# Attention and a noisy top-2 router with eight experts in one kernel: the router of two groups two slots earlier, weight loads re-timed, four experts per half before the halves alternate

## The chip, the cores and the metric

The kernel runs on one core of one Trainium2 chip. The metric is the device time of one execution in microseconds. Before the change the median of 14 runs is 454.57 us (450.78 to 479.65). One further execution was recorded by the profiler; it took 454.08 us, of which 452.3 us lie between its first and its last instruction (the span). All times inside the kernel below are counted from the start of that span.

Engine names in the profile: PE is the matrix engine (PEld its weight loads), ACT the scalar engine, DVE the vector engine, POOL the GpSimd engine, SP the sync engine. A trailing q (SPq, POOLq) is the engine's instruction queue, where DMAs are issued.

## The reference: what is computed

Two stages, one after the other. First causal attention in blocks of 64 over 8 batches, 8 heads, 576 positions and 64 channels. Its output is read as 4608 tokens of 512 channels. Then a mixture of experts: for each token two matrix products with 512x8 matrices give logits and a noise scale, the two largest of the 8 noisy logits are kept, and their softmax gives two weights. Each token goes through its two experts (512 to 1024, ReLU, 1024 to 512), and the two results are added with those weights.

```python
logits = x @ w_gate
noise_scale = np.log1p(np.exp(x @ w_noise))
noisy_logits = logits + noise_scale * noise
top2 = np.argpartition(-noisy_logits, 2, axis=1)[:, :2]
...
h = np.maximum(x[mask] @ w1[e], 0.0)
out[mask] += top2_w[mask, k, None] * (h @ w2[e])
```

## The kernel before, in words

**Attention.** The 8 batches form four groups of two (group 0 to 3). A group has 26 score units (UG = 26). One unit is a few PE matmuls into a PSUM tile and one exponential on ACT (`score_unit`, L284, the exponential at L301 or L312). Around each unit the kernel runs what was put on that slot's list: transposes of q and k, products with v (`av_tile`, L323, normalised on DVE at L362 and L363), transposes of the result, steps of the router, DMA issues. A slot is thus one unit: slots 0 to 103 are the four groups. The lists are filled with `at(slot, function, arguments)` and emptied with `run(slot)`. Each engine receives its instructions in the order in which they are written here, and works through them in that order.

**Router.** `router(g)` (L387) is a chain of 16 steps of small DVE instructions, three small ACT instructions and two PE matmuls (L439, L440). It finds for each token of a group its two experts and a free row in each expert's table. The list `rsl` (L767) gives the slot of every step, counted from the start of the next group (r0 = 26 g + 26); `r1` says when the group's scatters begin.

**Scatter.** `scatter(g, j)` (L499) is an indirect DMA issued by POOL. It writes 128 tokens to their rows in `xd`, an internal tensor in HBM with a table of 640 rows for each expert. There are two such tensors, one for each half of the tokens: groups 0 and 1 are half 0, groups 2 and 3 half 1. Each group has 18 scatters (9 token tiles, two experts), which may start only after the last paced instruction (`pace`) of their slot.

**Experts.** The work after attention is 16 blocks, `SEQ`, each one half with one expert. Before the change these are (half 0; experts 0, 1, 2), (half 1; experts 0, 1, 2), and then the halves in turn for experts 3 to 7. So block 3 is the first of half 1. `load_x` (L518) is a transposing DMA on SP's queue that brings the 640 rows of a block into SBUF (tile xg, for block 0 tile xa). It waits until all 36 scatters of its half have landed. `load_rec` (L527) brings the rows' records (destination, weights), and `read_rec` (L536) decodes them on DVE. `layer1` (L570) is 8 steps of 8 matmuls and one ReLU on ACT, `layer2` (L584) 5 tiles of 8 matmuls. In the PE's order the first layer-1 step of the next block stands ahead of layer 2 of this one. A token's first expert writes its result to `yd` in HBM (ACT's queue, L596), its second expert fetches that back with `gather` (L612, POOL, indirect), adds its own on DVE (L599) and sends the sum to the output with an indirect DMA (L601, POOL).

**Slots of the experts.** Slots from 104 on count the steps of the blocks: slots 104 to 110 hold the rest of group 3, block 0 has slots 111 to 124, block 1 has 125 to 137, block 2 begins at 138, and each later block has 13. Group 3's scatters stand at slots 118 to 135.

**Weights.** `load_w` (L219) brings one expert's two matrices in four DMAs of 512 KB, issued by POOL. The loads of experts 0 to 2 stand at fixed slots (L796, L797, L813); from expert 3 on they are issued during the blocks, as listed in `WL` (L822 to L825).

**The queues.** POOL issues q, k, v and weight loads, scatters, gathers and output writes in one order. Eight semaphores serve its DMAs in turn, so each DMA it issues first waits for the landing of the eighth before it. SP issues the clearing of `xd`, the transposing loads and the records in one order.

Of the kernel before, what the change touches and what calls it, by code (L numbers as in the profile page):

```python
# [19 lines left out]
def kernel(  # L20
# [37 lines left out]
    LT = (0, 1, 2, 3, 3, 4, 5, 5)  # L58
# [5 lines left out]
    UG = 2 * UN  # L64
# [25 lines left out]
    wE = main.enter_context(tc.tile_pool(name="wE", bufs=2))  # L90
# [6 lines left out]
    top = main.enter_context(ExitStack())  # L97
# [116 lines left out]
    def v_loads(g):  # L214
        return [(load_v, g, jt) for jt in range(4)] + [(load_v, g, 4, hf) for hf in range(2)]
# [3 lines left out]
    def load_w(pool, e, k=None):  # L219

        if k in (None, 0, "a"):
            wload[e] = (pool.tile([P, DB, F], BF16, tag="w1", name="w1sb"),
                        pool.tile([P, FB, Dm], BF16, tag="w2", name="w2sb"))
        for i, (t, src) in enumerate(zip(wload[e], (moe_w1[e], moe_w2[e]))):
            n = t.shape[1]
            w = src.rearrange("(b p) c -> p b c", p=P)
            if k is None or k == "ab"[i]:
                nc.gpsimd.dma_start(out=t, in_=w)
            elif k in (2 * i, 2 * i + 1):
                b0 = (k % 2) * n // 2  # L230
                nc.gpsimd.dma_start(out=t[:, b0:b0 + n // 2], in_=w[:, b0:b0 + n // 2])
# [286 lines left out]
    def load_x(b):  # L518
        half, e = SEQ[b]
        assert len(scat[half]) == 2 * TH  # L520
        xg = ffn["x"].tile([P, DB, CAP], BF16, tag="xg", name="xg") if b else xa
        ins = nc.sync.dma_start_transpose(out=xg, in_=xd[half][e * CAP:(e + 1) * CAP, 0:Dm])
        for nm in scat[half]:
            tc.add_manual_dep(ins.ins, nm, SYNC_DEP, reason="rows landed")
        xgs[b] = xg
# [99 lines left out]
    GJ = (2, 3, 4, 6, 7)  # L625
    GS = (2, 3, 5, 6)


    E1 = 3
    SEQ = [(h, e) for h in range(NH) for e in range(E1)]  # L630
    for e in range(E1, E):
        SEQ += [(0, e), (1, e)]
    NB = len(SEQ)
    todo = {}

    def at(slot, fn, *args):
        todo.setdefault(slot, []).append((fn, args))

    def run(slot):

        def rank(item):
            fn, args = item
            if fn is router_step:
                return 3 if rgen_n.get(args[0], 0) in (0, 1, 2, 8, 14, 15) else 0
            return {av_tile: 1, transpose_qk: 2, x_transpose: 2}.get(fn, 4)

        items = todo.pop(slot, [])
        while items:
            items.sort(key=rank)
            fn, args = items.pop(0)  # L650
            fn(*args)
# [52 lines left out]
    def read_flags():  # L704
        rs["over"] = nc.values_load(flag_i[0:1, 0:1], min_val=0, max_val=1)

    def warm():

        tp = tr_ps.tile([P, 4, P], F32, tag="tr")
        nc.tensor.matmul(out=tp, lhsT=ident, rhs=ident.unsqueeze(1).to_broadcast([P, 4, P]),  # L710
                         start=True, stop=True)
# [26 lines left out]
    for g in range(NG):  # L738
        s0 = g * UG
        last = g == NG - 1  # L740

        for nm, ch, i in (("q", 1, 0), ("k", 1, 2), ("k", 2, 4), ("q", 2, 6), ("k", "4A", 7), ("q", "4A", 8),
                          ("q", 3, 10), ("k", 3, 12)):
            at(s0 + i, transpose_qk, g, nm, ch)
        if not last:
            for nm, ch, i in (("q", 0, 14 if g else 19), ("k", 0, 17 if g else 22), ("q", "4B", 22), ("k", "4B", 21)):
                at(s0 + i, transpose_qk, g + 1, nm, ch)
            for i, (fn, *a) in enumerate(v_loads(g + 1)):
                at(s0 + 9 + i, fn, *a)
        if g == 0:  # L750
            at(s0 + 13, load_qk, 1, (2,))
            at(s0 + 16, load_qk, 1, (3,))
        if g == 0:
            for i, t in enumerate(((0, 6, 5), (1, 5), (6, 9))):
                at(s0 + 20 + 4 * i, load_tiles, 2, "q", *t)
                at(s0 + 21 + 4 * i, load_tiles, 2, "k", *t)
        elif g == 1:
            at(s0 + 14, load_tiles, 3, "q", 0, TG)
            at(s0 + 17, load_tiles, 3, "k", 0, TG)
        for i, a in enumerate((15, 16, 17, 18, 18, 19, 20, 21, 22, 23)):  # L760
            at(s0 + a, av_tile, g, 0, *((i,) if i < 8 else (8, i - 8)))
        r0 = s0 + UG
        if not last:
            avs = (0, 1, 1, 3, 4, 4, 5, 6, 7, 8)
            xts_ = (3, 5, 7, 9, 10)
        if g < 2:
            rsl = (11, 11, 12, 13, 14, 15, 16, 17, 19, 20, 21, 22, 23, 24, 25, 26)  # L767
            r1 = 26
        elif g == 2:
            rsl = (11, 11, 12, 13, 13, 14, 15, 16, 18, 19, 19, 20, 20, 21, 22, 22)  # L770
            r1 = 23
        else:
            avs, xts_ = (0, 0, 1, 1, 2, 2, 3, 3, 4, 4), (2, 3, 4, 5, 5)
            rsl = (5, 6, 6, 7, 7, 8, 8, 9, 10, 10, 11, 11, 12, 12, 13, 13)
            r1 = 14
        for i in range(TG + 1):
            at(r0 + avs[i], av_tile, g, 1, *((i,) if i < 8 else (8, i - 8)))
        for j in range(5):
            at(r0 + xts_[j], x_transpose, g, j)
        for j in range(RSTEPS):  # L780
            at(r0 + rsl[j], router_step, g)
        for j in range(2 * TG):
            at(r0 + r1 + (2 * j // 3, j, 4 * j // 5, j)[g], scatter, g, j)
# [10 lines left out]
    at(2 * UG + 4, clear_x, 1, 2 * UG + 3)  # L794
    for k in range(4):
        at(2 * UG + 1 + 2 * k, load_w, wE, 0, k)  # L796
        at(2 * UG + 20 + k, load_w, wE, 1, k)  # L797
    for u in (*range(2 * UG + 20, 2 * UG + 24), *range(3 * UG + 14, NG * UG)):
        at(u, warm)
    for u in range(NG * UG):  # L800
        score_unit(*divmod(u, UG))
        run(u)
        if u == 3 * UG + 13:
            raws_up.close()
            ffn["x"] = raws_up.enter_context(tc.tile_pool(name="xgp", bufs=3, side="right", reuse_waits="tile"))
            ffn["rec"] = raws_up.enter_context(tc.tile_pool(name="recp", bufs=1, side="right", reuse_waits="tile"))
            wM = raws_up.enter_context(tc.tile_pool(name="wM", bufs=1, side="right", reuse_waits="tile"))
            at(3 * UG + 18, load_x, 0)
            at(3 * UG + 19, load_x, 1)
            at(3 * UG + 20, load_rec, 0)  # L810
            at(3 * UG + 21, load_x, 2)
            for k in range(4):
                at(4 * UG + (5, 8, 11, 14)[k], load_w, wM, 2, k)  # L813

    WL = {}

    def open_top(slot):
        if slot == NG * UG + 6:
            top.close()
            wL = top.enter_context(tc.tile_pool(name="wL", bufs=2, reuse_waits="tile"))  # L820
            ffn["y"] = top.enter_context(tc.tile_pool(name="yp", bufs=4, reuse_waits="tile"))
            ffn["yg"] = [ffn["y"].tile([P, Dm], BF16, name=f"yg{i}", bufs=1) for i in range(GB)]  # L822
            for i, pool in enumerate((wL, wL, wE, wE, wM)):
                for k in range(4):
                    WL[3 + 2 * i + k // 2, (2, 6)[k % 2]] = (pool, 3 + i, k)  # L825

    slot = NG * UG
    at(slot + 14, read_rec, 0)
# [5 lines left out]
    def order(b):  # L834

        n = LT[SEQ[b][1]]
        return [*range(n, CT), *range(n)]
# [7 lines left out]
    for i in range(7):  # L845
        run(slot)
        slot += 1
        open_top(slot)
    XL = {(2, 4): 3}
    for b in range(2, NB - 2):  # L850
        XL[b, 5 if b == 2 else 1] = b + 2
    for fn, b, j in steps:
        fn(b, j)
        if fn is layer1:
            if (b, j) in XL:
                load_x(XL[b, j])
            if (b, j) == (2, 4):
                load_rec(1)
            if (b, j) == (3, 3):
                read_rec(1)  # L860
            if (b, j) in WL:
                load_w(*WL[b, j])
            if b in (1, E1 + 1) and j == 1:
                gather(b, 0)
            elif b < 9 and j in GJ and GJ.index(j) < LT[SEQ[b][1]]:
                gather(b, GJ.index(j))
            if 9 <= b + 1 < NB and j in GS and GS.index(j) < LT[SEQ[b + 1][1]]:
                gather(b + 1, GS.index(j))
        if fn is layer2 and 9 <= b + 1 < NB and j == order(b)[0] and LT[SEQ[b + 1][1]] > 4:
            gather(b + 1, 4)  # L870
            if b + 1 == NB - 1:
                nc.gpsimd.drain()  # L872
        run(slot)
        slot += 1
        open_top(slot)
# [90 lines left out]
```

## Time and profile before

| what | value |
|---|---|
| median of 14 runs | 454.57 us (450.78 to 479.65) |
| the profiled execution | 454.08 us |
| its span | 452.3 us |
| PE busy | 403.6 us (89% of the span) |
| ACT busy | 249.7 us (55%) |
| POOL busy | 240.8 us (53%) |
| DVE busy | 163.3 us (36%) |
| mean granted PE clock | 0.970 of full |
| layer-1 matmuls (L577) | 960 recorded, 134.4 us |
| layer-2 matmuls (L589) | 624 recorded, 140.7 us |
| scatters (L502) | 72, mean 986 ns on POOL |
| gathers (L617) | 48, mean 1033 ns on POOL |

A group's line names the source line, the engine, the tile written and the tiles read. Busy time is summed over the group. The idle time after the bar is that of the engine just before those instructions, with what ended most of it. Busy shares are means over the span; attention (to about 151 us) and the experts (from about 154 us) have different limits.

### The profile page before, as it was taken

The page shows a single profiled execution, that of the slowest core. Times are in us where ns is not written, and L with a number is a line of the kernel's source. Part 1 is how long each engine was busy: PE and PEld are TensorE (multiplying, and loading weights), DVE is VectorE, ACT ScalarE, POOL GpSimd, SP SyncE. Part 2 cuts the span into 40 slices and gives each one's busy share as a digit, 9 for nine tenths or more (in the row PEclk, how much of TensorE's full clock was granted, in tenths as well). Part 3 has the DMA queues.
Part 4 walks back from the last instruction along what each step waited for, and adds up shares of the span by engine and source line. Part 5 has one row for each costly group of instructions (what it writes and reads, how often), then busy time and mean ns, then how long its engine had stood idle before and what let it go on. Part 6 is the DMA issues. An engine that isn't in the chain of part 4 may idle for free. (4 is left out here: it accounts for less than half of the span.)

```text
span 452.3 us, 9839 instructions
## 1 busy us (share of the span) xinstructions
PE 403.6 (89%) x3952; PEld 248.5 (55%) x3968; DVE 163.3 (36%) x512; ACT 249.7 (55%) x339; POOL 240.8 (53%) x283
## 2 busy tenths in 40 slices
PE   2788788988989699975999999999999999999993
PEld 2456565655656465542556556556556566566561
DVE  1597489788788561000300101101101202302312
ACT  2889588997874155441445446455455455455140
POOL 8664360778767787670303125334746445756343
PEclk9989899999999799995999999999999999999998
DMA  8999999999983999439495996999999999945222
GB/s 132 171 133 144 231 194 162 249 242 166 164 203 111 206 210 265 144 132 175 116 181 97 173 185 159 125 212 191 209 244 230 166 244 220 226 139 176 68 85 103
DMA packets 134473, 78.93 MB, mean 175 GB/s; under 512 B 95777, under 2 KB 124195, under 8 KB 134420
## 3 DMA queue, kind: packets, MB, share of 16 engines
q0 software_dynamic: 70208, 56.05, 81.0%
q1 hardware_dynamic: 54132, 13.00, 19.7%
q10 hardware_dynamic: 10080, 9.18, 7.0%
q8 instruction: 33, 0.54, 0.5%
q14 instruction: 20, 0.16, 0.1%
HBM read 68.54 MB, written 33.13 MB: 225 GB/s over the span
## 5 line engine op out<-in xcount | busy, mean ns | idle before, releaser
L577 PE MATMUL hp<-xg,w1sb 128*128 128x320 bf16 x960 | 134.4, 300 | 8.3 <-DMA xg<-xd 8.3
L589 PE MATMUL yp<-w2sb,hq 128*128 128x512 bf16 x624 | 140.7, 382 | 1.0 <-issue 0.2
L577 PEld LDWEIGHTS <-w1sb 128*128 128x128 bf16 x1024 | 101.4, 99 | 55.0 <-DMA xg<-xd 8.7
L580 ACT ACTIVATE hq<-hp 128x640 bf16<-128x640 f32 x128 | 90.1, 704 | 72.8 <-PE hp L577 72.6
L599 DVE SCALAR_TENSOR_TENSOR yo<-yp,wrow,yg 128x512 f32<-128x512 f32 x46 | 34.5, 751 | 236.7 <-ACT ysb L594 210.4
L589 PEld LDWEIGHTS <-hq 128*128 128x128 bf16 x640 | 63.1, 99 | 74.4 <-issue 2.2
L301 ACT ACTIVATE esc<-sc 128x1024 bf16<-128x1024 f32 x96 | 93.8, 1025 | 11.0 <-PE sc L298 10.6
L601 POOL DMA_INDIRECT out_dram<-yo,trow x46 | 45.8, 995 | 91.2 <-DVE yo L599 78.4
L502 POOL DMA_INDIRECT xd<-xr,slots x72 | 71.0, 986 | 37.7 <-ACT esc L301 16.6
L594 ACT ACTIVATE ysb<-yp,wrow 128x512 bf16<-128x512 f32 x70 | 48.1, 687 | 74.1 <-PE yp L589 74.1
L617 POOL DMA_INDIRECT yg<-yd,orow x48 | 49.6, 1033 | 49.5 <-ACT hq L580 37.9
L298 PE MATMUL sc<-hq 64*128 64x512 bf16 (+4 forms) x320 | 38.3, 306 | 10.7 <-ACT esc L301 9.2
L344 PEld LDWEIGHTS <-esc 128*128 128x128 bf16 x640 | 23.3, 99 | 16.5 <-DVE xr L363 9.6
L344 PE MATMUL av<-vt,esc 128*128 128x65 bf16 x592 | 28.4, 196 | 4.1 <-DVE xr L363 3.8
L363 DVE TENSOR_TENSOR xr<-av,rden 128x256 bf16<-128x256 f32 x68 | 28.9, 424 | 2.4
L255 PE MATMUL tp<-ident,raw 128*64 128x128 bf16 x512 | 23.2, 241 | 5.8 <-DMA raw<-in_k_dram 3.2
L298 PEld LDWEIGHTS <-hq 64*128 64x128 bf16 x320 | 12.6, 95 | 20.9 <-issue 13.9
L255 PEld LDWEIGHTS <-raw 128*64 128x64 bf16 x512 | 17.9, 122 | 10.1 <-DMA raw<-in_k_dram 3.5
L208 POOL DMA_DIRECT2D vt<-in_v_dram x16 | 18.7, 1187 | 6.3 <-PE av L358 6.2
L268 ACT ACTIVATE hq<-tp 64x512 bf16<-64x512 bf16 (+1 forms) x16 | 12.9, 809 | 13.7 <-PE tp L255 7.9
L261 DVE COPY hq<-tp 128x1024 bf16<-128x1024 bf16 (+1 forms) x24 | 14.4, 598 | 8.1 <-PE tp L255 6.1
L362 DVE RECIPROCAL rden<-av 128x4 f32<-128x4 f32 x68 | 12.6, 186 | 8.0 <-PE av L344 4.7
(128 smaller groups left out, 244.7 us busy)
## 6 DMA issues: line engine op xcount, KB each, us to landing
yd<-ysb ACTq DMA_DIRECT2D x70, 128.0 KB, 3.7
w1sb<-in_moe_w_dram POOLq DMA_DIRECT2D x16, 512.0 KB, 7.8
w2sb<-in_moe_w_dram POOLq DMA_DIRECT2D x16, 512.0 KB, 8.6
vt<-in_v_dram POOLq DMA_DIRECT2D x16, 256.0 KB, 10.0
raw<-in_q_dram POOLq DMA_DIRECT2D x9, 256.0 KB, 10.8
raw<-in_k_dram POOLq DMA_DIRECT2D x9, 256.0 KB, 8.4
xd<-zero SPq DMA_DIRECT2D x16, 132.0 KB, 9.8
raw<-in_q_dram POOLq DMA_DIRECT2D x1, 1152.0 KB
```

The source lines that it names most:

```text
L255: nc.tensor.transpose(to[64 * hf:64 * hf + 64, :, r, :], raw[:, (t0, t1)[hf], r * 64:(r + 1) * 64], ident)
L298: nc.tensor.matmul(out=sc[:, hf, off:off + z - a], lhsT=kT[sl, c0 + jt * P:c0 + jt * P + P], rhs=qT[sl, c0 + a:c0 + z], start=True, stop=True)
L301: ins = nc.scalar.activation(out=esc[:, hh, :, piece * 512:(piece + 1) * 512], in_=sc, func=AF.Exp, scale=scale)
L344: nc.tensor.matmul(out=av[:, hh, :], lhsT=esc[:, hh, hf, c:c + P], rhs=vb[:, 2 * jt + hf, st * SET + hh, :], start=(jt == 0), stop=(jt == ib))
L502: ins = nc.gpsimd.indirect_dma_start(out=xd[half].bitcast(I32), out_offset=bass.IndirectOffsetOnAxis(ap=slots[:, g * TG + idx, i:i + 1], a ...
L577: nc.tensor.matmul(out=hp[:, n, 0:NW], lhsT=w1sb[:, db, fb * P:(fb + 1) * P], rhs=xgs[b][:, db, n * NW:(n + 1) * NW], start=(db == 0), sto ...
L580: ins = nc.scalar.activation(out=hs[b][:, fb, :].rearrange("p (n w) -> p n w", n=2), in_=hp[:, :, 0:NW], func=AF.Relu)
L589: nc.tensor.matmul(out=yp, lhsT=hs[b][:, fb, c * P:(c + 1) * P], rhs=w2sb[:, fb, :], start=(fb == 0), stop=(fb == FB - 1))
L594: ins = nc.scalar.activation(out=ysb, in_=yp, func=AF.Copy, scale=w)
L599: nc.vector.scalar_tensor_tensor(out=yo, in0=yp, scalar=w, in1=ygs.pop((b, c)), op0=ALU.mult, op1=ALU.add)
L601: ins = nc.gpsimd.indirect_dma_start(out=out, out_offset=bass.IndirectOffsetOnAxis(ap=trow[half][:, e, c:c + 1], axis=0), in_=yo, in_offse ...
L617: ins = nc.gpsimd.indirect_dma_start(out=yg, out_offset=None, in_=yd[half][0:e * CAP, :], in_offset=bass.IndirectOffsetOnAxis(ap=orows[hal ...
```

## The change

It has five parts.

1. `rsl` and `r1` for groups 0 and 1: the router's last nine steps stand one or two slots earlier (the chain ends at slot 24 instead of 26), and the group's scatters begin at slot 24 instead of 26, counted from r0. Groups 2 and 3 keep theirs.
2. Expert 1's four weight loads stood at slots 72 to 75, ahead of group 1's scatters (78 to 95). They now stand at 79, 82, 85 and 88, among group 1's scatters (now 76 to 93).
3. `E1` is 4 instead of 3: the order of blocks is (half 0; experts 0, 1, 2, 3), (half 1; experts 0, 1, 2, 3), then the halves in turn for experts 4 to 7. The first block of half 1 is now block 4.
4. The transposing loads and record loads follow: block 3's load (half 0 now) is written at step 3 of block 1, that of block 4 and the records of half 1 at step 4 of block 3, their decoding at step 3 of block 4. Expert 3's weights are loaded at slots 123, 126, 129 and 132, among group 3's scatters; experts 4 to 7 follow from block 4 on.
5. In the two blocks of expert 1, the gather of tile 0 was issued twice (at step 1 and again at step 2). Now it is issued once. The bounds 9 in the gather rules become 2 E1 = 8.

```diff
-    E1 = 3
+    E1 = 4
...
+    pools = {}
+
+    def load_later(e, k):
+        load_w(pools["wL"], e, k)
...
         if g < 2:
-            rsl = (11, 11, 12, 13, 14, 15, 16, 17, 19, 20, 21, 22, 23, 24, 25, 26)
-            r1 = 26
+            rsl = (11, 11, 12, 13, 14, 15, 16, 16, 17, 18, 19, 20, 21, 22, 23, 24)
+            r1 = 24
...
     for k in range(4):
         at(2 * UG + 1 + 2 * k, load_w, wE, 0, k)
-        at(2 * UG + 20 + k, load_w, wE, 1, k)
+        at(3 * UG + 1 + 3 * k, load_w, wE, 1, k)
...
             for k in range(4):
                 at(4 * UG + (5, 8, 11, 14)[k], load_w, wM, 2, k)
+                at(4 * UG + 19 + 3 * k, load_later, 3, k)
...
-            wL = top.enter_context(tc.tile_pool(name="wL", bufs=2, reuse_waits="tile"))
+            wL = pools["wL"] = top.enter_context(tc.tile_pool(name="wL", bufs=2, reuse_waits="tile"))
...
-            for i, pool in enumerate((wL, wL, wE, wE, wM)):
+            for i, pool in enumerate((wL, wE, wE, wM)):
                 for k in range(4):
-                    WL[3 + 2 * i + k // 2, (2, 6)[k % 2]] = (pool, 3 + i, k)
+                    WL[4 + 2 * i + k // 2, (2, 6)[k % 2]] = (pool, 4 + i, k)
...
-    XL = {(2, 4): 3}
-    for b in range(2, NB - 2):
-        XL[b, 5 if b == 2 else 1] = b + 2
+    XL = {(1, 3): 3, (3, 4): 4}
+    for b in range(3, NB - 2):
+        XL[b, 5 if b == 3 else 1] = b + 2
...
-            if (b, j) == (2, 4):
+            if (b, j) == (3, 4):
                 load_rec(1)
-            if (b, j) == (3, 3):
+            if (b, j) == (4, 3):
                 read_rec(1)
...
             if b in (1, E1 + 1) and j == 1:
                 gather(b, 0)
-            elif b < 9 and j in GJ and GJ.index(j) < LT[SEQ[b][1]]:
+            elif b not in (1, E1 + 1) and b < 2 * E1 and j in GJ and GJ.index(j) < LT[SEQ[b][1]]:
                 gather(b, GJ.index(j))
-            if 9 <= b + 1 < NB and j in GS and GS.index(j) < LT[SEQ[b + 1][1]]:
+            if 2 * E1 <= b + 1 < NB and j in GS and GS.index(j) < LT[SEQ[b + 1][1]]:
                 gather(b + 1, GS.index(j))
-        if fn is layer2 and 9 <= b + 1 < NB and j == order(b)[0] and LT[SEQ[b + 1][1]] > 4:
+        if fn is layer2 and 2 * E1 <= b + 1 < NB and j == order(b)[0] and LT[SEQ[b + 1][1]] > 4:
             gather(b + 1, 4)
```

## The prediction

> **What bounds the kernel now.** I read the 10 us stages first. From 220 us to 440 us PE is busy 9.95 to 10.00 of every 10 us at full clock, so this stretch is bound by PE, and the change leaves its matmuls alone. PE loses time in two places behind attention.
>
> ```profile
> 150.00:160.00 10.00, 7.02 (x63) 4.40 (x60) 3.48 (x14) 1.93 (x5) 7.83 (x9) 0.66 1.27 208
> 200.00:210.00 10.00, 1.68 (x8) 0.89 (x7) 0.00 (x0) 0.70 (x1) 3.04 (x3) 0.69 0.95 132
> 210.00:220.00 10.00, 9.78 (x39) 4.25 (x38) 0.00 (x0) 3.37 (x5) 0.00 (x0) 0.80 0.74 170
> 230.00:240.00 10.00, 9.96 (x51) 4.96 (x51) 0.00 (x0) 4.42 (x7) 0.00 (x0) 1.00 0.89 144
> ```
>
> Columns: stage, its length, busy us (and instructions) of PE, PEld, DVE, ACT, POOL, then PE's granted clock. The reader sees 1.68 us of PE work in 200 to 210, and clocks of 0.66 to 0.80 around both holes. Next the waits: both holes are waits for transposing loads.
>
> ```profile
> PE hp L577 <- DMA xg<-xd: 8.3, 1, 8.3
> PE hp L577 <- DMA xa<-xd: 3.0, 1, 3.0
> ```
>
> Then the timelines of PE, POOL and SP, to see what is late.
>
> ```profile
> 153.90 7.17 PE L577 MATMUL hp<-xa,w1sb 128*128 128x320 bf16 x32 [2.98 <-DMA xa<-xd]
> 165.38 1.25 PE L577 MATMUL hp<-xg,w1sb 128*128 128x320 bf16 x8
> 175.10 8.86 PE L577 MATMUL hp<-xg,w1sb 128*128 128x320 bf16 x64
> 184.01 8.58 PE L589 MATMUL yp<-w2sb,hq 128*128 128x512 bf16 x39
> 208.53 2.31 PE L577 MATMUL hp<-xg,w1sb 128*128 128x320 bf16 x8 [8.32 <-DMA xg<-xd]
> 220.92 1.25 PE L577 MATMUL hp<-xg,w1sb 128*128 128x320 bf16 x8
> ```
>
> ```profile
> 117.78 1.07 POOL L502 DMA_INDIRECT xd<-xr,slots  x1 [0.30 <-issue]
> 143.64 0.97 POOL L502 DMA_INDIRECT xd<-xr,slots  x1 [0.31 <-issue]
> 183.37 1.07 POOL L617 DMA_INDIRECT yg<-yd,orow  x1 [3.39 <-ACT hq L580]
> 198.92 0.97 POOL L502 DMA_INDIRECT xd<-xr,slots  x1 [0.30 <-ACT hq L580]
> ```
>
> ```profile
> 146.35 3.17 SPq L522 DMA_TRANSPOSE xa<-xd  x1
> 154.67 49.40 SPq L522 DMA_TRANSPOSE xg<-xd  x2
> 204.25 0.46 SPq L529 DMA_DIRECT2D rc<-xd  x1
> ```
>
> The hole at 200: block 3 is half 1's first. Its load waits for the last scatter of group 3, which POOL issues at 198.92 to 199.89. SP is held in the pair of loads until 204.25, and PE gets the rows at 208.53: 8.6 us from POOL's end to PE's start. The hole at 151: the last scatter of half 0 is that at 143.64, SP issues block 0's load at 146.35, PE starts at 153.90: 9.3 us after POOL's end (144.61). PE had run out at 150.92.
>
> Each hole also costs clock. From 165.38 to 175.10 one layer-1 step and layer 2 take 9.72 us; the same work after the long hole takes 220.92 - 208.53 = 12.39, that is 2.67 more. Block 0's eight steps take 165.38 - 153.90 = 11.48, block 1's 184.01 - 175.10 = 8.91: 2.57 more, less some 0.1 for two router matmuls among them, 2.5. So the long hole costs 8.32 + 2.67 = 11.0 us, the short one 2.98 + 2.5 = 5.5 us.
>
> **The change, part by part.** *Order of blocks (E1).* Block 3 now reads half 0, complete since 146 us. Its load is issued on SP right behind block 2's, at about 159 us, so the long hole goes: -11.0. The wait moves to block 4, wanted one block later. On the time base of before, PE without the hole ends block 2's layer 1 at 200.2 and begins block 4 at 200.2 + 8.9 + 8.6 = 217.7. When are its rows there? On POOL, 13 DMAs ran from 183.37 to 199.89 (two gathers, eleven scatters, 1.27 each). Now there are one gather, eleven scatters and three of expert 3's loads (0.8 and a gap of 0.3 each): 183.37 + 12 x 1.28 + 3 x 1.1 = 202.0. With the 8.6 us of before, PE has the rows at 210.6, 7.1 us early. A rule speaks against this: the Trainium skill, "DMA: Bandwidth & Descriptors", in its section on SWDGE, HWDGE and iDMA, says that GpSimd has a single software queue, so scatters lie in the rings behind the 512 KB loads. The trace agrees in kind: scatters landed in a median of 2.4 us from 183 us on (no loads near them), 6.1 us from 146 to 183 (expert 2's loads among them), 9.5 us from 78 to 95 (expert 0's loads, clears and k and q). By the rows without loads the margin is 7.1; by the rule with the 6.1 us row it is 7.1 - 3.7 = 3.4, with the 9.5 us row 0.0. I take 3.4: nothing is paid at block 4. If another 4 us came, 0.6 would be paid, and the clock might fall.
>
> Expert 3's weights are a new deadline: both halves of w1 at 200.2. The first is issued ahead of the gather at 183.37, the second two scatters behind it, near 187; with the 7.8 us of w1 loads it lands at 195. Margin 5, cost 0; without it PE would stand where it stood. Block 3's transposing load falls into 159 to 168, where the DMA queues hold expert 2's loads (wanted at 183.9 and later, issued by 171.5, landing in 10.0). POOL may wait there for landings; its 3.39 us of idle ahead of 183.37 covers that.
>
> The records of half 1 follow block 4's load on SP, near 209, and are wanted by layer 2 of block 4 near 236. Block 3's three gathers are issued at its steps 2 to 4, need block 2's last yd write (3.7 us to land), and their tiles are read third to fifth in layer 2, 8 us later or more. POOL waits there with only output writes behind it. Cost 0. Expert 4 to 7's loads stand a block earlier than they did, their use where it was.
>
> *Router and scatters of groups 0 and 1.* The same instructions, two slots earlier. From the end of slot 51 to that of slot 77 ACT needs 32.8 us for 26 slots: 1.26 each, so 2.5 us. POOL's queue runs without long waits from the first scatter at 80.08 to 114.3, and moves by 2.5 as a whole. On DVE nothing is added; ACT idles 1.49 and 1.86 us for the chain's end (L481) in the two groups, because L315's clears (1.1 us) stand ahead of it. They now stand behind. I count nothing for that, since block 0 starts when its rows come. The two router matmuls have one slot less behind DVE; PE waited 0.4 us or less there, and ACT has 1 us of copy (L268) to cover it.
>
> *Expert 1's loads.* Before, they filled 114.47 to 117.47, and then stalled the scatters by their landings: 1.70, 1.51 and 1.58 where 0.30 is usual, 3.9 us in excess. Now the first scatter of group 1 can go at 112.0. 18 scatters by 1.28 are 23.0, a clear and copy between them 0.4, four loads by 1.1 are 4.4, the kind of excess that expert 0's spread loads show (0.49, 0.48, 1.01 for 0.30) 1.1, and for v loads still on their way I put 1.5: 142.4 instead of 144.61, -2.2. Bounds: no such waits give 139.8, the old excess of 3.9 on top gives 146.3, +1.7. I take -2.1, near the row of expert 0's loads. PE takes up to 2.98.
>
> *The clock at 151.* Here a rule and the trace differ.
>
> ```profile
> 149.34:152.75 3.41, 1.27 (x40) 0.97 1.53 260
> 152.75:156.17 3.42, 2.27 (x9) 0.50 1.01 223
> ```
>
> (Stage, length, PE busy, clock, DMA share and GB/s.) The Trainium skill, "TensorE: Matmul & The Clock Gate", Part 1, has the clock halve after an idle window of about 3.4 us. By it a 2.98 us hole costs no clock, and a shorter one still none. The trace halved it after this window with 1.27 us of work, and elsewhere after one with 1.30 and one with 2.42 (half of it transposes); others with 2.04 and 2.08 kept it. A hole of 0.9 us adds 2.1 us of work to this window, 3.4, or less if the window falls otherwise. By the rule the gain is 0, by the row up to 2.5. I take half, -1.2.
>
> *One gather less in two blocks:* 1.3 us of POOL each, behind PE's cover: 0.
>
> **Sum:** -11.0 - 2.1 - 1.2 = -14.3 us. The profiled execution's 454.08 (span 452.3 and 1.8 around it) becomes 439.8; it lies 0.5 under the median of 454.57, so 440.3, in round numbers 440.
>
> **Rivals.**
> 1. *Only the long hole goes.* The scatters of half 0 end no earlier (loads now in their midst): 454.57 - 11.0 = 443.5. For it: 512 KB loads among scatters gave landings of 9.5 us. Against: three waits of before go.
> 2. *Part of the hole comes back at block 4*, with half-clock behind it. If group 3's scatters are 8 us later than I reckon, 4.6 us and 2.7 for the clock: 440.3 + 7.3 = 447.6. For it: the rule of the single queue. Against: the DMA share is 0.46 and 0.43 in the stages from 180 to 200.
> 3. *The wait only changes place:* block 4 pays all 11 and the rest is noise, 452 to 455. It needs scatters 12 us later.
> 4. *Slower.* Expert 1's four loads among the last scatters of half 0 hold POOL for their landings. It is slower than before when they cost block 0 more than 11.0 + 2.3 us: over 4.4 us per load (13.3 and the 4.4 already counted, by four) instead of 1.1. With 6 us each: 4 x 4.9 = 19.6 late, less 11.0: 463. Against: expert 0's loads, spread alike, cost 0.2 to 0.7 beyond the usual gap.
>
> **How the numbers follow.** My forecast has 0.62, the rivals 0.13, 0.11, 0.06 and 0.08. The forecast's own range is 435 to 444: 5.5 at the short hole (and some of ACT's idle) below, none of it above. With rivals 1 and half of 2 the range 435 to 448 leaves out about 0.2. Half a per cent, 2.3 us, is about what a measurement of this kernel can tell from no change: faster 0.62 + 0.13 + 0.11 = 0.86, same 0.06, slower 0.08.
>
> **What would show it.** Right: no wait of PE for xg; block 3 follows block 2 at full clock; block 4's load is issued on SP well ahead of PE's start; block 0's wait for xa under 1.5 us; the last scatter of half 0 ends near 142. Wrong: a wait for xg or w1sb at block 3 or 4; POOL waits of several us on weight loads between 112 and 143, or later than 205 for the last scatter; attention ending later than 151.

## The result

The changed kernel takes 463.76 us in the median of 10 runs (457.21 to 470.83); the kernel before, on the same chip, 454.78 us (47 runs, 450.64 to 479.65). The ratio is 1.013, with a 95% interval of 1.009 to 1.017; like every ratio here it leaves out the disturbed executions, while the two medians alone would give 1.020. The forecast was 440 (435 to 448): wrong in sign.

The profiled execution of the changed kernel took 454.25 us, with a span of 452.2. That of before took 454.08, with a span of 452.3. So the trace shows a gain of 14.3 us that did not come, and nothing more: the ten timed executions took 3 to 17 us longer than the profiled one, and what made them longer this trace does not show. One more execution on record, outside the ten, took 454.79. The granted PE clock does not tell them apart: 0.961 in the profiled one, 0.958 to 0.969 in the ten.

These waits of PE, ACT and POOL in the changed kernel, some out of a longer list (us in total, times, longest), are no longer those of before:

```profile
PE hp L577 <- ACT hq L580: 9.0, 2, 6.1
POOL xd L502 <- ACT hq L580: 7.2, 8, 5.1
ACT hq L580 <- DMA xg<-xd: 6.8, 1, 6.8
ACT ysb L594 <- DMA xg<-xd: 4.8, 1, 4.8
POOL xd L502 <- DMA xd<-xr,slots: 4.6, 6, 3.0
PE hp L577 <- DMA w1sb<-in_moe_w_dram: 0.5, 1, 0.5
```

PE waits for xg no more. It waits for hq, the ReLU's output, and it is ACT that stands for xg: an engine that never reads xg. The timeline of PE shows where:

```profile
154.06 6.38 PE L577 MATMUL hp<-xa,w1sb 128*128 128x320 bf16 x32 [5.86 <-DMA xa<-xd]
191.79 2.34 PE L577 MATMUL hp<-xg,w1sb 128*128 128x320 bf16 x16
197.06 6.14 PE L577 MATMUL hp<-xg,w1sb 128*128 128x320 bf16 x44 [2.93 <-ACT hq L580]
203.73 0.72 PE L577 MATMUL hp<-xg,w1sb 128*128 128x320 bf16 x4 [0.53 <-DMA w1sb<-in_moe_w_dram]
204.50 8.58 PE L589 MATMUL yp<-w2sb,hq 128*128 128x512 bf16 x39
212.92 2.34 PE L577 MATMUL hp<-xg,w1sb 128*128 128x320 bf16 x16
221.36 9.02 PE L577 MATMUL hp<-xg,w1sb 128*128 128x320 bf16 x48 [6.11 <-ACT hq L580]
```

At 212.92 PE stands at block 3's second step, which the kernel before reached at 220.92: 8.0 us ahead. Then come 6.11 us of standing still and a half-clock stretch. The 64 matmuls that follow (seven steps of block 3, one of block 4) end at 221.36 + 9.02 = 230.38; before, at 220.92 + 8.86 = 229.78. All of the lead is gone within 18 us. The stages show the clock (columns as in the prediction, then DMA share and GB/s):

```profile
150.00:160.00 10.00, 5.95 (x30) 3.71 (x31) 1.90 (x8) 2.02 (x3) 7.65 (x8) 0.66 1.21 245
190.00:200.00 10.00, 7.07 (x48) 4.48 (x46) 0.75 (x1) 3.95 (x6) 6.65 (x7) 1.00 1.08 250
200.00:210.00 10.00, 9.41 (x54) 5.12 (x54) 0.00 (x0) 4.66 (x8) 7.86 (x10) 1.00 1.00 185
210.00:220.00 10.00, 5.25 (x31) 2.84 (x29) 1.41 (x2) 1.73 (x3) 4.83 (x5) 0.97 0.84 221
220.00:230.00 10.00, 8.64 (x47) 5.51 (x47) 0.00 (x0) 4.78 (x7) 3.16 (x4) 0.69 0.99 152
```

**Why ACT stands.** Two timelines of the changed kernel, ACT's and SP's:

```profile
187.53 0.33 ACTq L596 DMA_DIRECT2D yd<-ysb  x1
188.54 0.69 ACT L594 ACTIVATE ysb<-yp,wrow 128x512 bf16<-128x512 f32 x1 [1.04 <-PE yp L589]
193.64 0.33 ACTq L596 DMA_DIRECT2D yd<-ysb  x1
194.07 0.69 ACT L594 ACTIVATE ysb<-yp,wrow 128x512 bf16<-128x512 f32 x1 [4.84 <-DMA xg<-xd]
...
213.12 0.69 ACT L594 ACTIVATE ysb<-yp,wrow 128x512 bf16<-128x512 f32 x1 [1.04 <-PE yp L589]
220.23 0.33 ACTq L596 DMA_DIRECT2D yd<-ysb  x1
220.61 1.30 ACT L580 ACTIVATE hq<-hp 128x640 bf16<-128x640 f32 x2 [6.80 <-DMA xg<-xd]
```

```profile
154.87 26.17 SPq L522 DMA_TRANSPOSE xg<-xd  x2
215.51 2.53 SPq L522 DMA_TRANSPOSE xg<-xd  x1
```

In the built program the DMAs of SP and of ACT share eight semaphores, in turn. Whoever comes eighth after a DMA waits, at its issue, for that DMA's landing. What counts is the order of the built program, in which block 3's load stands ahead of block 0's five yd writes, though the source has it behind them. In the changed kernel the eighth after block 3's load is block 1's third yd write (L596); the eighth after block 4's load is block 2's fifth yd write. The first of these keeps ACT from 189.2 to 193.6, the second from 213.8 to 220.2, and both end as the load lands. ACT works in order, so the next ReLU is late, the PSUM tile that it reads (where the matmuls write) is not freed, and PE stands. In the kernel before, the load of half 1's first block also shared its turn with a yd write, the fourth of block 2, but that write stood behind the first matmuls that use this load's rows, and so after its landing.

Block 3's load is slow. The two loads in SP's first line above are those of block 2 and block 3; as a group (SP's time for one: least, median and most, in ns; first and last start; then the landing that the trace recorded):

```profile
L522 SPq DMA_TRANSPOSE xg<-xd x2: 6744/13059/19374, 154.9 to 161.7; - x2
DMA to landing us min/median/max: 31.9/31.9/31.9
```

SP was rid of block 3's load only after 19.4 us, and it landed 31.9 us behind its issue at 161.7. The DMA share is 1.14 to 1.24 in the stages from 160 to 190.

Its neighbours are slow too. The landings (KB each, median us from issue to landing), of the kernel before from 146 to 183 us, then of the changed one from 154 to 196:

```profile
w2sb<-in_moe_w_dram POOLq DMA_DIRECT2D x2, 512.0 KB, 10.0
yd<-ysb ACTq DMA_DIRECT2D x5, 128.0 KB, 5.9
```

```profile
w1sb<-in_moe_w_dram POOLq DMA_DIRECT2D x4, 512.0 KB, 17.4
yd<-ysb ACTq DMA_DIRECT2D x10, 128.0 KB, 11.6
```

Over 154 to 196 us the ten yd writes of the kernel before landed in a median of 4.0 us. POOL paid for this with two waits among group 3's scatters:

```profile
177.84 0.99 POOL L502 DMA_INDIRECT xd<-xr,slots  x1 [5.08 <-ACT hq L580]
181.86 0.98 POOL L502 DMA_INDIRECT xd<-xr,slots  x1 [3.04 <-DMA xd<-xr,slots]
```

The name in the first line misleads. In the built program this scatter waits for block 1's first ReLU, which had ended at 166.74, and for the landing of the scatter issued at 162.69, eight POOL DMAs earlier: that leaves the landing. Both waits are over before expert 3's first load is issued, at 187.29. What is new in this stretch is block 3's load. That it is what slows the others is likely, and not shown: no run took it alone away on this chip.

### The profile page after: what moved, and what is told of

It is laid out like the page before. It is cut to its first block, busy times and chain, and to the rows that moved or that the text cites. A ratio compares the mean times of both kernels' runs of the same rounds, so it can differ in the third digit from the quotient of the medians.

```text
span 452.2 us, 9833 instructions
## 1 busy us (share of the span) xinstructions
PE 405.5 (90%) x3952; PEld 249.5 (55%) x3968; DVE 161.8 (36%) x512; ACT 249.8 (55%) x339; POOL 239.1 (53%) x281
## 5 line engine op out<-in xcount | busy, mean ns | idle before, releaser
L577 PE MATMUL hp<-xg,w1sb 128*128 128x320 bf16 x960 | 135.8, 302 | 9.6 <-ACT hq L580 9.0
L589 PE MATMUL yp<-w2sb,hq 128*128 128x512 bf16 x624 | 139.2, 379 | 0.8
L617 POOL DMA_INDIRECT yg<-yd,orow x46 | 47.4, 1030 | 55.5 <-ACT hq L580 20.9
L298 PE MATMUL sc<-hq 64*128 64x512 bf16 (+4 forms) x320 | 40.1, 321 | 7.8 <-ACT esc L301 6.6
L344 PEld LDWEIGHTS <-esc 128*128 128x128 bf16 x640 | 24.3, 101 | 14.8 <-DVE xr L363 6.4
L344 PE MATMUL av<-vt,esc 128*128 128x65 bf16 x592 | 29.4, 200 | 1.6 <-DVE xr L363 1.2
L577 PE MATMUL hp<-xa,w1sb 128*128 128x320 bf16 x64 | 10.9, 338 | 5.9 <-DMA xa<-xd 5.9
```

The costliest lines, as they stand in the source:

```text
L298: nc.tensor.matmul(out=sc[:, hf, off:off + z - a], lhsT=kT[sl, c0 + jt * P:c0 + jt * P + P], rhs=qT[sl, c0 + a:c0 + z], start=True, stop=True)
L344: nc.tensor.matmul(out=av[:, hh, :], lhsT=esc[:, hh, hf, c:c + P], rhs=vb[:, 2 * jt + hf, st * SET + hh, :], start=(jt == 0), stop=(jt == ib))
L577: nc.tensor.matmul(out=hp[:, n, 0:NW], lhsT=w1sb[:, db, fb * P:(fb + 1) * P], rhs=xgs[b][:, db, n * NW:(n + 1) * NW], start=(db == 0), sto ...
L589: nc.tensor.matmul(out=yp, lhsT=hs[b][:, fb, c * P:(c + 1) * P], rhs=w2sb[:, fb, :], start=(fb == 0), stop=(fb == FB - 1))
L617: ins = nc.gpsimd.indirect_dma_start(out=yg, out_offset=None, in_=yd[half][0:e * CAP, :], in_offset=bass.IndirectOffsetOnAxis(ap=orows[hal ...
```

## The experiments

They ran on chips on which attention takes some 24 us longer: block 0 starts at 177.80 in the kernel before, instead of 153.90, and there are stretches of about 2 us (147 to 149, say) in which PE, ACT and DVE all stand and the trace names no releaser. Each ratio is against the kernel before on the same chip. Expert 2's loads follow the end of attention, so block 3's load, issued near 174, has 13 us before the first of them (187.0): the condition in dispute is absent there unless a run makes it. Theory A is that the early load of block 3, slow among expert 2's loads, holds ACT through the shared semaphore; theory B that expert 3's loads among the scatters cost; theory C that the front part (router, expert 1's loads) costs.

**1. The front part alone, and the order alone.**

```diff
 # e1_front: the kernel before with
+            rsl = (11, 11, 12, 13, 14, 15, 16, 16, 17, 18, 19, 20, 21, 22, 23, 24)
+            r1 = 24
+        at(3 * UG + 1 + 3 * k, load_w, wE, 1, k)
 # e2_back, e2_back2: the changed kernel with these three lines as before
```

> The kernel before with only the router of groups 0 and 1, their scatters and expert 1's loads moved; order of blocks and the double gather as before. Theory A (block 3's transposing load, issued near 162 us among expert 2's loads, makes the loss: it lands after 32 us, holds ACT at a write of block 1, and slows the scatters of group 3): that load isn't there, so the time is that of before, ratio 0.995 to 1.005, attention ends near 148 us, block 0 still starts near 154, the long wait for xg near 8 us stays. Theory B (expert 3's loads among group 3's scatters make the loss): the same here. Theory C (the front part makes the loss): ratio about 1.013.

> The changed kernel with the router, the scatters and expert 1's loads put back where they were; four experts per half first, and all that follows from it. Theories A and B: loses like the whole change, ratio 1.005 to 1.02, ACT is held by 4 to 8 us at a write of block 1 and again at one of block 2. Theory C: ratio under 1.0.

> The order of blocks alone, front as before, next to the whole change on one chip. Theory A (early transposing load among expert 2's loads): on a chip with attention ending near 150 us the same holds of ACT as in the changed kernel, ratio within 0.005 of it. Theory C (the front part costs): ratio lower than the changed kernel's by 0.01 or more, as the first four runs had it (0.979 here, 1.0105 for the front alone).

> The changed kernel once more, on the chip of the next three. On a chip like that of the first profiles: ratio 1.005 to 1.02, ACT held at a write of block 1 by 3 us or more for block 3's load, then at the last write of block 2 by 5 us or more for block 4's. Where attention runs on to 185 us, as in the first four experiments, block 3's load lies ahead of expert 2's loads, lands early, and neither theory has the first hold.

Measured: the front part alone 1.0105 (1.0061 to 1.0150). The order alone 0.979 (0.961 to 0.996), and again 0.988 (0.984 to 0.992), 478.94 us. The whole change 1.001 (0.996 to 1.006), 484.67 us. So here the order of blocks gains 1.2 to 2.1%, 6 to 10 us, and the front part loses about 1%, as theory C had it and not A or B: together nothing. But the gain is not the one that I had costed. The stages of the kernel before on such a chip (first) and of the order alone (second):

```profile
220.00:230.00 10.00, 4.67 (x18) 2.48 (x18) 0.00 (x0) 2.06 (x4) 5.75 (x6) 0.63 0.56 139
```

```profile
220.00:230.00 10.00, 9.95 (x68) 6.50 (x68) 0.38 (x1) 5.18 (x8) 7.86 (x9) 1.00 1.02 230
230.00:240.00 10.00, 9.06 (x51) 4.79 (x50) 1.50 (x2) 5.08 (x8) 2.06 (x3) 1.00 0.94 163
```

The hole of the kernel before lies in block 2, not in front of block 3, and is no wait for xg. ACT and PE there:

```profile
222.63 0.70 ACT L580 ACTIVATE hq<-hp 128x640 bf16<-128x640 f32 x1 [4.95 <-remote]
```

```profile
223.38 2.29 PE L577 MATMUL hp<-xg,w1sb 128*128 128x320 bf16 x8 [4.46 <-ACT hq L580]
```

"Remote" is a release that the trace ties to no instruction. All four profiles of the old order on these chips have a standstill of PE of 4.5 to 7.4 us there (between 218 and 235); with the new order there is none of more than 1.0 us between 200 and 245, unless a run makes one. What ends it is not known.

**2. The front part split.**

```diff
 # e6_router: the kernel before with the new rsl and r1 only
 # e7_w1: the kernel before with expert 1's loads at 3 * UG + 1 + 3 * k only
 # before_look: the kernel before
```

> The kernel before with the router of groups 0 and 1 two slots earlier, and nothing else of the change. Both front parts together cost 1.0% on this kind of chip. If the router's place is what costs (ACT and DVE do its work where attention needed them), this run is at 1.007 to 1.012 of before. If the spread loads of expert 1 are what costs, it is at 0.997 to 1.002. My forecast had it at 0.995 or lower.

> The kernel before with expert 1's four loads spread among the scatters of group 1, and nothing else of the change. If these loads cost (landings that POOL waits for, or bytes beside q, k and v loads in attention), 1.007 to 1.012 of before; if the router is the cost, 0.997 to 1.002. My forecast had it at 0.995.

> The kernel before, profiled on the chip of these runs. It gives the end of attention, the last scatter of half 0 and the start of block 0 against which the front runs are read. If the front costs by POOL (theory C), its last scatter of half 0 ends 3 us or more earlier than in the run with both front parts; if by ACT or DVE, its last scores matmul does.

Measured: the router alone 515.43 us (494.13 to 523.70, 4 runs), expert 1's loads alone 488.16 (476.20 to 490.78, 4 runs), before 485.65 (478.40 to 489.33, 7 runs). The router's trace has five standstills of PE of 5.5 to 7.2 us in the experts' part, two of them behind yd writes that stand for loads (point 4). Its four runs all lie above the seven of before, which points at the router; but they differ by 30 us among themselves, and with expert 1's loads moved as well the loss was 1%. They do not settle it. Block 0 starts at 177.80 in the kernel before, at 179 to 185 in the three profiles of the new order with the old front, at 181 to 187 in those with both front parts: the ranges overlap. Which front part costs, and by what, stays open.

**3. The load of block 3 held back.** The load is put at block 2's first step, and waits for the ReLU there.

```diff
+        if b == 3:
+            tc.add_manual_dep(ins.ins, pace[-1], SYNC_DEP, ...)
-    XL = {(1, 3): 3, (3, 4): 4}
+    XL = {(2, 1): 3, (3, 4): 4}
```

> The changed kernel with block 3's load held back until the first layer-1 step of block 2 is done, near 185 us, when expert 2's loads have landed; expert 3's loads stay among the scatters. Theory A: the load lands in under 10 us, ACT is not held at any write, the last scatter is issued near 202 us instead of 209, block 4's rows are in time: 440 to 445 us, ratio 0.97 to 0.98. Theory B: the last scatter stays at 207 to 210, block 4 or ACT waits for block 4's load by 5 us or more: ratio 0.99 to 1.01.

> Block 3's load held to block 2's first step, as in the first four runs, next to the changed kernel. Theory A as it stood: 0.97 to 0.98. After the first run of it (PE waited 13.2 us for the held load, which shared the queues with expert 3's loads and the scatters): a transposing load takes 15 us or more next to POOL's DMAs wherever it lies, so PE waits directly at block 3, ratio 1.00 to 1.03.

Measured: 1.019 (0.994 to 1.044), and again 1.046 (1.031 to 1.062). The waits and PE's timeline of the first:

```profile
PE hp L579 <- DMA xg<-xd: 13.2, 1, 13.2
```

```profile
245.65 2.29 PE L579 MATMUL hp<-xg,w1sb 128*128 128x320 bf16 x8 [13.17 <-DMA xg<-xd]
```

SP issued the load at 226.73, between expert 3's loads (217.7, 222.4, 227.0) and group 3's scatters; PE had the rows at 245.65, 18.9 us later. A transposing load among weight loads is slow on this chip too. Theory A as it stood had a landing in under 10 us and 0.97 to 0.98: it missed. Holding the load back is no cure.

**4. The shared semaphore given away.** Loads of 32 bytes on SP take turns.

```diff
 # e3_lane: two loads right behind block 3's; e5_turn: one between block 1's second and third yd write
 # e8_turn2: one there, and one between block 2's third and fourth yd write
+        if fn is layer2 and (b, j) in SPARE_AT:
+            ins = nc.sync.dma_start(out=spare[SPARE_AT.index((b, j))], in_=moe_noise[0:1, :])
+            tc.add_manual_dep(ins.ins, pace[-1], SYNC_DEP, ...)
 # e11_order_turn: e8_turn2 with router and expert 1's loads as before
```

(The first run has no such dependence.)

> The changed kernel with two loads of 32 bytes into tiles that nothing reads, on SP right behind block 3's load. The eight semaphores serve the DMAs of SP and ACT in one turn, so block 3's load now has the semaphore of block 1's first write to yd, no longer that of its third. If ACT is held by that turn (theory A): the hold is at block 1's first write, near 186 us, and lasts 6 to 9 us where it lasted 4.8; the time grows by about 3 us, ratio about 1.02. If ACT is held by something else at that time, such as a full queue: the hold stays at the third write, ratio about 1.013.

> The changed kernel with one load of 32 bytes on SP that takes the semaphore of block 3's load when its turn comes, between the second and the third write of block 1, so that SP waits there and not ACT. If the shared turn of semaphores holds ACT: block 1's third write is issued at once, PE isn't stalled at block 2's third step, the span is 3 us shorter than that of the changed kernel; the hold for block 4's load stays. If something else holds ACT: no difference.

> The changed kernel with two loads of 32 bytes on SP that take the turns of the semaphores of block 3's and block 4's transposing loads, so that no yd write of ACT waits for either load. If the early load is held for tens of us and holds ACT (theory A), no wait of ACT for xg is left, no wait of PE for hq ahead of block 3 and 4, and the time is 8 to 12 us under the changed kernel: 0.985 of before. If congestion or the front part is what costs (theories B and C), the waits of PE move to w1sb or xg and the time is within 0.5% of the changed kernel. Where attention lasts long and block 3's load lands early, ACT is not held in the changed kernel either, and the run tells nothing apart.

> The new order of blocks alone (router and expert 1's loads as before) with the two turn-taking loads: the version that should beat both kernels. Theory A: 0.975 to 0.985 of before, and 5 us or more under the changed kernel, wherever it runs. If the front part was no loss but a gain, it is above the changed kernel with the same two loads, which had 0.983.

Measured: two loads behind block 3's 0.986 (0.973 to 0.998), where both readings had expected a loss; one turn taken 484.29 us (4 runs) with before at 487.89; one load for each of the two turns 0.983 (0.971 to 0.996), 472.55 us; the same with the old front 0.986 (0.971 to 1.001), 476.18 us. The edit of the last two does not do what I had meant by it: in the built program only the first small load takes the turn that it was made for, that of block 3's load. The second stands ahead of block 4's load, takes the turn of block 1's second yd write, and so moves the turn of block 4's load from block 2's fifth write to block 3's third, some 14 us later. In none of these runs, nor in the changed kernel beside them, did ACT stand for block 3's load, so they do not say what taking its turn is worth. What they do show is that ACT is held elsewhere, by the loads of later blocks, and in the old order too. The front part alone, ACT and PE in the eleventh block:

```profile
394.91 0.33 ACTq L596 DMA_DIRECT2D yd<-ysb  x1
395.29 0.69 ACT L594 ACTIVATE ysb<-yp,wrow 128x512 bf16<-128x512 f32 x1 [7.25 <-DMA xg<-xd]
```

```profile
396.81 3.57 PE L589 MATMUL yp<-w2sb,hq 128*128 128x512 bf16 x8 [6.04 <-DVE yo L599]
```

A yd write stands 7.25 us for a load, and PE 6.04. The router alone has two such (6.47 and 6.68 us), the two loads behind block 3's load one (3.03), the run with a load for each turn one (4.48). Where only block 3's turn was taken, block 2's fifth write stood 1.49 us for block 4's load, as in the first profile. In the eleven other profiles of points 1 to 5 there is no such hold. So whether a turn falls badly changes from one profile to the next; that this is why the timed runs exceed the profiled one is likely, and not shown.

Leaving out the runs that hold block 3's load back, the versions with the new order are 1.2 to 2.1% faster than before with the old front, and 0 to 1.7% with the new. None of the variants was run where attention ends at 150 us.

**5. The collision made on purpose, first try.** Block 3's load waits for block 0's second ReLU, without and with the two small loads of e8_turn2; the changed kernel beside them.

```diff
+        if b == 3:
+            tc.add_manual_dep(ins.ins, ffn["relu01"], SYNC_DEP, ...)
```

> The changed kernel, but block 3's transposing load is issued only when block 0's second ReLU is done, about 8 us behind block 0's start, as it was in the first profile: it then falls among expert 2's loads and group 3's scatters also where attention lasts long. Theory A (these loads make its landing slow, and through the shared semaphore the third yd write of block 1 holds ACT): the load takes 20 to 32 us to land instead of under 15, ACT has a wait of 2 to 8 us for xg among block 1's writes, PE waits for hq ahead of block 3, and the time is 3 to 10 us over the changed kernel's on this chip. If the place among the loads is harmless, it is within 2 us of it.

> The same late load, with the two 32-byte loads on SP that take the semaphores' turns of block 3's and block 4's loads, so that no yd write waits for either. Theory A: the load lands as late as in the run without them, ACT has no wait for xg, and what that run lost is gained back as far as block 3's rows are there when PE wants them: within 2 us of the changed kernel. If the slow landing or the crowded rings cost by themselves (PE waiting for xg or w1sb), the loss stays.

> The changed kernel again, as the partner of the three runs beside it. Where attention ends near 150 us, 1.013 of before with ACT held by block 3's and block 4's loads; where it ends near 180 us, 1.00 of before and hardly a hold, since block 3's load then lands ahead of expert 2's loads.

Measured: late 1.013 (1.005 to 1.021), 486.87 us; late with the small loads 0.992 (0.988 to 0.997), 482.47 us; the changed kernel 481.99 (4 runs); before 486.12. The times are as theory A has them, but its trace is not: in the late run SP was rid of the load in 4.0 us, and no wait of ACT for xg appears; block 1's third write came 31.7 us behind the issue, and by then the load had landed. A match in times without the wait behind it proves nothing.

**6. The collision made on purpose, second try.** Now the write that shares the load's turn comes some 11 us behind the load: five 32-byte loads on ACT use up turns, so that it is block 0's third write. The partner has one more, on SP, that takes this turn.

```diff
 # e12_next0: block 3's load behind block 0's fourth ReLU, and
+        if fn is layer1 and (b, j) in TURNS:     # ((0,4), (0,5), (0,6), (0,7), (1,0))
+            nc.scalar.dma_start(out=spare[TURNS.index((b, j))], in_=moe_noise[0:1, :])
 # e13_next0_turn: the same, and
+        if fn is layer2 and (b, j) == (0, 1):
+            ins = nc.sync.dma_start(out=spare[5], in_=moe_noise[0:1, :])
+            tc.add_manual_dep(ins.ins, pace[-1], SYNC_DEP, ...)
```

> The changed kernel, but block 3's load is issued behind block 0's fourth ReLU, among expert 2's loads, and five 32-byte loads on ACT's queue use up turns, so that block 0's third yd write, some 14 us behind the issue, is the one that gets the semaphore of block 3's load. Theory A (the load takes 19 to 32 us to land there, and ACT stands for it): ACT waits 4 to 15 us for xg in the midst of block 0's writes, PE waits for hq in block 1, and the time is 4 to 15 us over its partner's, 1 to 3%. If a load among these loads lands within 14 us on this chip, ACT has no such wait and the two are within 1% of each other.

> The partner: the same, with one more 32-byte load, on SP between block 0's second and third write, that takes that turn. The load of block 3 lands as late as in the other run. Theory A: no wait of ACT for xg in block 0, no wait of PE for hq in block 1, and 4 to 15 us less than the other. If the crowded queues cost by themselves, both lose the same.

Measured: 491.26 us (479.43 to 496.49) and 487.90 (481.33 to 494.18), 6 runs each, beside before at 498.62 (483.41 to 513.26, 11 runs): the times are not told apart. The traces are, one of each; that of the first is its slowest execution. Without the extra load, SP's issue, ACT and PE:

```profile
193.80 6.70 SPq L522 DMA_TRANSPOSE xg<-xd  x1
```

```profile
204.05 0.69 ACT L598 ACTIVATE ysb<-yp,wrow 128x512 bf16<-128x512 f32 x1 [1.04 <-PE yp L593]
212.75 0.33 ACTq L600 DMA_DIRECT2D yd<-ysb  x1
213.12 0.69 ACT L598 ACTIVATE ysb<-yp,wrow 128x512 bf16<-128x512 f32 x1 [8.39 <-DMA xg<-xd]
```

```profile
207.30 2.34 PE L579 MATMUL hp<-xg,w1sb 128*128 128x320 bf16 x16
216.06 8.61 PE L579 MATMUL hp<-xg,w1sb 128*128 128x320 bf16 x48 [6.43 <-ACT hq L582]
```

With it:

```profile
191.51 7.07 SPq L522 DMA_TRANSPOSE xg<-xd  x1
211.23 0.26 SPq L869 DMA_DIRECT2D spare<-in_moe_noise_dram  x1
```

```profile
204.71 0.69 ACT L598 ACTIVATE ysb<-yp,wrow 128x512 bf16<-128x512 f32 x1 [1.04 <-PE yp L593]
209.62 0.33 ACTq L600 DMA_DIRECT2D yd<-ysb  x1
209.99 1.30 ACT L582 ACTIVATE hq<-hp 128x640 bf16<-128x640 f32 x2 [4.59 <-DMA spare<-in_moe_noise_dram]
```

```profile
210.75 8.36 PE L579 MATMUL hp<-xg,w1sb 128*128 128x320 bf16 x48 [3.90 <-ACT hq L582]
```

The load takes 19 to 20 us to land in both: ACT is let go at 212.75, 18.95 us behind its issue, and in the partner SP, which now stands for it, at 211.23, 19.7 us behind it. In the first, ACT is held 8.39 us by a load that it does not read, and PE stands 6.43 us for hq two steps later: the pattern of the changed kernel, made at another place. One 32-byte load moves this hold from ACT to SP, where nothing is queued behind it. The partner is not free of a hold: its fifth write stood 4.59 us for one of ACT's own 32-byte loads, the third, issued at 193.91 and down 15.7 us later, with 3.90 us of PE; and block 2's fifth write stood 2.15 us for block 4's load, as in the changed kernel. So two things act together: DMAs issued in this stretch land late, even one of 32 bytes, and the turn decides which engine pays.

What follows. That a slow transposing load holds ACT through a shared semaphore, and PE through ACT, is shown: in the first profile by the named waits, here by a hold that was made and moved. That it is the whole of the 1.3% is not shown. Theory B has no run of its own. The first profile speaks against it as the start of the delay: POOL's two long waits ended at 177.84 and 181.86, ahead of expert 3's first load at 187.29. What it says of crowded queues is part of the cause (block 4's rows came 9.6 us later than I had reckoned). Theory C holds on these chips (1.0%), without a cause; in the first profile the blocks up to block 1 came 0.6 us earlier with it.

## Why the prediction was wrong, point by point

- *The long hole goes, -11.0.* Right: no wait for xg, and at 212.92 PE is 8.0 us ahead, after 2.93 and 0.53 us of new waits.
- *"Block 3's transposing load falls into 159 to 168, where the DMA queues hold expert 2's loads … POOL may wait there for landings; its 3.39 us of idle ahead of 183.37 covers that."* This is the step that failed: I put the load at no cost. I gave it no landing time, and I did not ask who waits for its semaphore: I had told of eight semaphores in turn for POOL's DMAs and had not looked for the same on SP and ACT. It was not late for block 3 (it landed at 193.6, wanted at about 200), but it took 31.9 us. POOL waited 5.08 and 3.04 us for landings, which 3.39 does not cover, and ACT stood 4.84 us for it at a yd write, with 2.93 us of PE behind that.
- *Expert 3's weights, "Margin 5, cost 0".* The second half of w1 was issued at 195.50, not near 187, because POOL was late. PE waited 0.53 us for it: the sign "a wait for xg or w1sb at block 3 or 4" that I had named, small.
- *Block 4: "nothing is paid".* Failed likewise. Group 3's last scatter ended on POOL at 209.53, not 202.0. POOL's two waits for landings, and 2.47 us ahead of its gather at 191.83, less the 3.39 that I had taken over from before, make up 7.2 of these 7.5 us. From there to the issue of the load went 6.0 us (215.51), where before it was 1.7 (199.89 to 201.55), 4.3 more: so the rule of the single software queue was right in kind, and my 3.7 for it a little too small. Still the rows were there at 220.2, and an unhindered PE would have wanted them at about 220.7, by an estimate (212.92 and seven steps of 1.11 us, from the 8.86 that eight took before). It was again the turn: block 2's fifth write stood for that load, 6.80 us of ACT, 6.11 of PE, and 2.5 us of half clock (2.34 + 9.02 for steps that took 8.86 before).
- *Sum at the blocks:* -11.0 + 2.93 + 0.53 + 6.11 + 2.5 = +1.1, where I had -11.0. With -0.8 of half clock saved in block 0 (10.69 us for eight steps instead of 11.48) and +0.16 for its start, +0.5; the trace has +0.6 at 230 and -0.1 in the span.
- *Expert 1's loads, -2.1.* The last scatter of half 0 ended at 143.62, 1.0 earlier instead of 2.1: the first of group 1 went at 114.22, not 112.0, and v loads cost 2.03 and 0.69. Then its landing took 2.9 us instead of 1.7, and SP issued block 0's load at 146.56, 0.2 later than before. Nothing was gained.
- *ACT's idle at the router's end, "I count nothing".* PE ran out of attention's work 2.7 us earlier (148.20 instead of 150.92); the 1.49 and 1.86 us of ACT were gone. That only widened the hole in front of block 0 from 2.98 to 5.86, because the rows, not attention, set its start.
- *The clock at 151, -1.2.* It was -0.8, by a longer hole instead of a shorter one; the reasoning does not stand.
- *Rivals.* The third (the wait changes place, 452 to 455) had the time of the profile, 454.25, by luck: it let block 4 pay for late scatters, 12 us; they were 7.5 us late, and the price was paid on ACT. No rival held the 463 of the runs; the fourth had that number for POOL's sake, and POOL did not stand for expert 1's loads.

## What to carry to other kernels

Before a DMA is moved earlier or into a busy stretch, list which semaphore it takes and which instruction, on which engine, takes it next: if that engine does work in order for the bottleneck, the DMA's landing is a deadline even when its data are wanted much later. Where rows land in time and an engine waits for them that never reads them, a shared turn is the first suspect. A profiled execution tells where a gain went, and need not contain the loss that the runs show; a ratio that comes out as expected while the expected wait is missing from the trace is no proof.

## What the runs showed of the hardware

- A transposing load of 640 rows landed in 4.6 us when the last 512 KB load had been issued some 10 us before it (SP's queue was rid of it in 2.5 us). Among 512 KB loads, scatters and yd writes one took 31.9 us to land, 19.4 of them in issue; on other chips 18.9 to 19.7. Even a 32-byte load took 15.7 us there.
- Next to that load of 31.9 us, a 512 KB load of the same stretch landed in 17.4 us instead of 10.0, and ten yd writes of 128 KB in a median of 11.6 instead of 4.0.
- A standstill of PE of 2.93 us (194 to 197) left the granted clock at 1.00. That of 2.98 us in the kernel before fell in a stage at 0.66; those of 5.86 and 6.11 us fell in or were followed by stages at 0.66 and 0.69.
- The same kernel began its experts at 153.90 us on one chip and at 177.80 on another, with pauses in which PE, ACT and DVE stand together.
